# Last batch of a feature attention and gated MLP: sums of squares at fixed addresses, last output product in fp32 halves

## The chip, the cores and the metric

One core of one Trainium2 chip. The metric is the device time of one execution in microseconds. Five engines work beside each other, each through its own instructions in order: PE (TensorE, matrix products from SBUF into PSUM banks), PEld (its loads of the stationary operand), DVE (VectorE), ACT (ScalarE), POOL (GpSimd), and SP (SyncE), which issues the transfers.

## What is computed

For 4 batches of 1088 rows: an attention with products of features, 4 heads of 32 columns, and behind it a gated MLP. Cut to what matters:

```python
def phi(x):                                  # r = 8, so 64 features
    a = einsum('rd,bhsd->bhsr', S1, x)
    b = einsum('rd,bhsd->bhsr', S2, x)
    return einsum('bhsi,bhsj->bhsij', a, b).reshape(..., 64)
kv = einsum('bhsf,bhsd->bhfd', phi(k), v)
z = sum(phi(k), axis=2)
x = einsum('bhsf,bhfd->bhsd', phi(q), kv) / (einsum('bhsf,bhf->bhs', phi(q), z)[..., None] + 1e-6)

h = maximum(x @ w_in, 0)                     # 128 -> 1024
u, v = h[..., :512], h[..., 512:]
v_n = (v - mean(v)) / sqrt(var(v) + 1e-6)
v_s = einsum('ts,bsd->btd', w_spatial, v_n) + b_spatial[None, :, None]
out = (u * v_s) @ w_out                      # 512 -> 128
```

## The kernel before

**Precision.** Nearly every fp32 operand is split into a high part and a low rest, both of the type fp32r, and a product is three fp32r products, hi·hi, lo·hi and hi·lo (mm3, lines 441 to 444). The split of a tile is a cast on ACT (line 521) and a difference on DVE (line 452) or POOL (line 455). Weights arrive as 64-bit floating numbers and are brought to fp32 by from_f64 (from line 485), one step on ACT and six on a vector engine.

**Stages.** The kernel runs attention(b) (line 716), hidden_v (line 789: the half v, normed, as vh, vl and a rest v9) and main(b) (line 847) for the four batches, overlapping. main works on blocks (d, c): d is one of ND = 4 groups of 128 of the 512 columns, c one of three pieces of the 1088 rows, PIECES = 424, 332 and 332 columns wide, which stand in wTh and wTl at columns 0, 448 and 780. A block has its half u (bank pu, line 948), the product with w_spatial (nine steps of 128 rows, line 963 and those behind it, in a bank sp), the gate (a DVE product, line 1000, then the split into g, or xh and xl, or r) and out_mm (line 926), which adds the block's part of the output into a bank po of its piece. When the four d are summed, the bank is copied and stored. PSUM has three po banks, two sp, one pu and two sd.

**The last batch.** It runs in the order (0,0), (1,0), (2,0), quad 0, quad 2, (3,0). quad(d0) (line 1121) computes the 2 x 2 blocks of d0 and d0+1 and pieces 1 and 2 with seven products in place of eight, from sums of parts of w_spatial (w_sums, line 1033; its 16 parts are loaded again) and sums of parts of v (s_stores, s_sums, from line 1075, numbered 1 to 4). prod, line 1147, is the PE product with them, 12 instructions each, 14 of them: 168 instructions. plus (line 1155) and more add banks and kept sums on DVE.

**Order.** The code lists operations; Order.schedule (from line 190) sorts them on each engine from due times that run back from the end, taking away an entry of the table LEADS (line 66) for each operation. Tiles of a tag share a few buffers in a fixed turn (SB_BUFS), so an operation can wait until the tile that had its buffer is done with. HOMES (line 51) lists, in groups, the order in which the buffers lie in SBUF; two of its groups begin at an address of 0 and 64 modulo 256 bytes. In the products of prod, vh, vl, wih and wil stand at 64, and wTh, wTl, xh, xl, c and r at 0; kp, kt, v and pl stand where they come to lie.

**The end.** In before, the last block (3,0) ends with the gate (DVE, 424 columns), the cast to g (ACT), the difference (DVE), three fp32r products of 424 columns into po, a copy (ACT, line 937) and the store (SP, line 942).

Of the kernel before, what the change touches and what calls it, by code (L numbers as in the profile page):

```python
# [19 lines left out]
P = 128  # L20
# [3 lines left out]
ND = DH // P  # L24
# [27 lines left out]
    ("eps", "mask_sb", "sk", "bh", "bl", "sm", "st", "mv", "abT", "ka", "u", "vt", "kp", "kt", "v", "pl"),  # L52
    (0, "wTh", "wTl", "xh", "xl", "g", "c", "r", "b32"),
    (64, "vh", "vl", "v9", "wih", "wil", "woh", "wol", "kvh", "kvl"),
# [314 lines left out]
def tile_kernel(ctx: ExitStack, tc: tile.TileContext, kT, qT, vA, sks, idn, msk, wT, w_in, w_out, bsp, out):  # L369
# [35 lines left out]
    def reserve():  # L405

        at, base = 1024 + 4 * 32, None

        def up(n):
            return -(-n // 32) * 32  # L410

        for group in HOMES:
            if not isinstance(group[0], str):
                base = at if base is None else base
# [70 lines left out]
    def from_f64(x32, raw, n):  # L485
# [31 lines left out]
        step(c1, lambda v: v.tensor_tensor(out=x(), in0=x(), in1=ev(), op=ALU.add), [(x32, "e")], [(x32, "x")])  # L517
# [271 lines left out]
    def hidden_v(b, st, g):  # L789
# [46 lines left out]
        small(lambda: nm.ap, lambda: mv[:, :, 0], -sign, lambda: rs.ap, ALU.mult, ALU.mult, [mv, rs], [nm])  # L836
        for t in range(3):
            def dve(t=t):
                v.tensor_scalar(out=vt[:, t], in0=vt[:, t], scalar1=mv[:, t, 0:1], scalar2=rs[:, t:t + 1], op0=ALU.add if by_act else ALU.subtract, op1=ALU.mult)  # L839

            def act(t=t):
                nc.scalar.activation(vt[:, t], vt[:, t], AF.Identity, bias=nm[:, t:t + 1], scale=rs[:, t:t + 1])

            op("DVE", c_dve2(DH, True), dve, r=[mv, rs, nm], w=[(vt, t)], sh=True, alts=[("ACT", c_act(DH, ptr=True), act)], kind=f"norm{b}")


    def main(b, st):
        po, sums = [None] * 3, [0] * 3
        wide = b == B - 1
# [73 lines left out]
        def out_mm(d, c, hi, lo, parts):  # L923
            c0, cw = cols[c]
            if po[c] is None:
                po[c] = bank("po", f"po{b}{c}")
            o = po[c]
            sums[c] += 1
            first, end = sums[c] == 1, sums[c] == ND
            op("PE", c_mm(cw, 3), lambda: mm3(o[:, :cw], woh[:, d], wol[:, d], hi(), lo(), start=first, stop=end), r=[*parts, woh, wol], w=[o], due=due(c_mm(cw, 3)))  # L930
            if end:
                ob = tl("vt" if wide else "kp" if big(c) else "u", f"ob{b}{c}", [P, cw])
                late = due(0)

                def copy(eng, at, n, key):
                    if eng == "ACT":
                        op("ACT", c_act(n, True), lambda: nc.scalar.copy(out=ob[:, at:at + n], in_=o[:, at:at + n]), r=[o], w=[(ob, key)], due=late, lead=-8000)
                    else:
                        op("DVE", c_dve(n), lambda: nc.vector.tensor_copy(out=ob[:, at:at + n], in_=o[:, at:at + n]), r=[o], w=[(ob, key)], due=late, lead=-8000)

                def store(at, n, r):
                    op("SP", 470, lambda: nc.sync.dma_start(out=out[b, :, c0 + at:c0 + at + n], in_=ob[:, at:at + n]), r=r, kb=n // 2, due=late, lead=-12000)


                copy("DVE" if wide and c == 1 else "ACT", 0, cw, 0)
                store(0, cw, [ob])
# [51 lines left out]
        def gate(d, c, sp, u):  # L998
            cw = cols[c][1]
            op("DVE", c_dve(cw), lambda: nc.vector.tensor_tensor(out=u.ap, in0=sp[:, :cw], in1=u.ap, op=ALU.mult), r=[sp], w=[u], lead=LEAD[1])  # L1000
            if big(c):
                g = tl(("xh", "xl")[d % 2], f"g{b}{d}{c}", [P, 2, WIDE], F32R)
                parts = [(lambda: g[:, 0, :cw], (g, 0)), (lambda: g[:, 1, :cw], (g, 1))]
            else:
                tag = "r" if last(d, c) else "g"
                gh, gl = tl(tag, f"gh{b}{d}{c}", [P, cw], F32R), tl(tag, f"gl{b}{d}{c}", [P, cw], F32R)
                parts = [(lambda: gh.ap, gh), (lambda: gl.ap, gl)]
            (hi, wh), (lo, wl) = parts
            split(hi, lo, lambda: u.ap, cw, [u], [wh], [wl])
# [79 lines left out]
        def s_sums(d0, stores):  # L1089
# [7 lines left out]
            for m in range(2):  # L1097
# [3 lines left out]
                def own(t, at):  # L1101
                    return (lambda: t[:, at]), t
# [149 lines left out]
        for args in late:  # L1252
            out_mm(*args)
# [78 lines left out]
```

## Time and profile before

| what | us |
|---|---|
| three runs | 337.47, 330.95, 329.16; median 330.95 |
| the profiled execution | 329.36 |
| its span | 327.6 |
| PE busy in the span | 320.1 (98%) |
| DVE, ACT, POOL busy | 229.7, 166.7, 66.9 |
| granted clock of TensorE | 0.999 of full speed |

The times of the rows count from the span's start; 1.76 us of the execution lie outside the span. In a row, the number behind the start is the duration, and brackets give how long the engine had been idle before and what released it.

### The profile page before, as it was taken

The page shows a single profiled execution, that of the slowest core. Times are in us where ns is not written, and L with a number is a line of the kernel's source. Part 1 is how long each engine was busy: PE and PEld are TensorE (multiplying, and loading weights), DVE is VectorE, ACT ScalarE, POOL GpSimd, SP SyncE. Part 2 cuts the span into 40 slices and gives each one's busy share as a digit, 9 for nine tenths or more (in the row PEclk, how much of TensorE's full clock was granted, in tenths as well). Part 3 has the DMA queues.
Part 4 walks back from the last instruction along what each step waited for, and adds up shares of the span by engine and source line. Part 5 has one row for each costly group of instructions (what it writes and reads, how often), then busy time and mean ns, then how long its engine had stood idle before and what let it go on. Part 6 is the DMA issues. An engine that isn't in the chain of part 4 may idle for free.

```text
span 327.6 us, 6711 instructions
## 1 busy us (share of the span) xinstructions
PE 320.1 (98%) x2579; PEld 304.0 (93%) x2579; DVE 229.7 (70%) x503; ACT 166.7 (51%) x390; POOL 66.9 (20%) x83
## 2 busy tenths in 40 slices
PE   8999999999999999999999999999999999999995
PEld 7887988899999899999899999999999999999994
DVE  4899997444699973689976579899325777267281
ACT  2589656535674654576535476552424554153241
POOL 1000011685111025420102902156000013012000
PEclk9999999999999999999999999999999999999999
DMA  7932149764020274101044214000000231000001
GB/s 192 329 102 68 53 138 306 236 191 136 3 69 20 52 247 140 42 2 48 21 123 128 62 46 147 3 15 29 0 2 0 83 112 42 0 3 0 0 3 68
DMA packets 21260, 26.69 MB, mean 81 GB/s; under 512 B 2796, under 2 KB 20972, under 8 KB 21228
## 3 DMA queue, kind: packets, MB, share of 16 engines
q1 hardware_dynamic: 21228, 26.26, 26.1%
q8 instruction: 20, 0.33, 0.4%
q14 instruction: 12, 0.10, 0.1%
HBM read 23.18 MB, written 3.06 MB: 80 GB/s over the span
## 4 chain that ended last, share of the span: by engine, by line
PE 77%; DVE 9%; DMA 7%; ACT 3%; SPq 2%; issue 1%; DVEq 0%
PE sp L963 16%; PE sp L965 14%; PE sp L972 14%; PE sd L1147 4%; DMA v<-in_vA 3%; PE sp L1147 3%; DMA pl<-in_wT 3%; PE sd L442 3%; PE sd L444 3%; PE sd L443 3%; PE pu L442 2%; PE po L443 2%; PE pu L443 2%; PE pu L444 2%; PE sp L974 2%; PE po L442 2%
## 5 line engine op out<-in xcount | busy, mean ns | idle before, releaser
L963 PE MATMUL sp<-wTh,vh 128*128 128x332 f32 (+1 forms) x350 | 114.7, 328 | 0.0
L965 PE MATMUL sp<-wTh,vl 128*128 128x332 f32 (+1 forms) x304 | 99.0, 326 | 0.0
L972 PE MATMUL sp<-wTl,vh 128*128 128x332 f32 (+1 forms) x304 | 97.1, 326 | 0.0
L963 PEld LDWEIGHTS sp<-wTh,vh 128*128 128x128 f32 x350 | 65.8, 188 | 2.1 <-issue 1.0
L965 PEld LDWEIGHTS sp<-wTh,vl 128*128 128x128 f32 x304 | 57.2, 188 | 0.6
L972 PEld LDWEIGHTS sp<-wTl,vh 128*128 128x128 f32 x304 | 57.1, 188 | 0.1
L1000 DVE TENSOR_TENSOR u<-sp,u 128x332 f32<-128x332 f32 (+1 forms) x44 | 23.0, 522 | 23.6 <-PE sp L974 17.2
L521 ACT CAST g<-u 128x332 fp32r<-128x332 f32 (+1 forms) x42 | 20.5, 490 | 34.5 <-DVE u L1000 18.5
L452 DVE TENSOR_TENSOR g<-u,g 128x332 fp32r<-128x332 f32 (+1 forms) x42 | 24.2, 576 | 18.4 <-PE po L443 11.6
L777 DVE RECIPROCAL c<-c 128x384 f32<-128x384 f32 (+1 forms) x9 | 21.8, 2418 | 17.5 <-ACT c L775 17.5
L955 ACT ACTIVATE u<-pu 128x332 f32<-128x332 f32 (+1 forms) x44 | 20.6, 468 | 24.0 <-PE pu L444 19.4
L879 ACT CAST vh<-vt 128x384 fp32r<-128x384 f32 x36 | 17.6, 511 | 17.4 <-DVE vt L839 8.5
L803 DVE BATCH_NORM_STATS2 st<-vt 128x6 f32<-128x512 f32 x36 | 24.3, 686 | 1.9 <-ACT vt L801 1.4
L455 POOL TENSOR_TENSOR r<-pl,r 128x384 fp32r<-128x384 f32 (+1 forms) x18 | 17.6, 985 | 39.0 <-ACT r L521 30.1
L801 ACT ACTIVATE vt<-sd 128x512 f32<-128x512 f32 x36 | 21.3, 599 | 6.6 <-PE sd L444 5.8
L746 POOL TENSOR_TENSOR pl<-pl,pl 128x384 f32<-128x384 f32 (+1 forms) x18 | 17.6, 988 | 33.7 <-DMA pl<-qd 31.7
L881 DVE TENSOR_TENSOR vl<-vt,vh 128x384 fp32r<-128x384 f32 (+1 forms) x36 | 19.1, 540 | 7.5 <-ACT vh L879 7.4
L442 PE MATMUL pu<-xh,wih 128*128 128x332 f32 (+1 forms) x48 | 16.3, 339 | 0.7 <-ACT kp L955 0.6
L565 ACT CAST wTh<-pl 128x332 fp32r<-128x332 f32 (+1 forms) x27 | 13.0, 497 | 7.6 <-DMA pl<-in_wT 7.3
L839 DVE TENSOR_SCALAR vt<-vt,mv,sm 128x512 f32<-128x512 f32 x33 | 16.2, 540 | 0.0
L443 PE MATMUL pu<-xl,wih 128*128 128x332 f32 (+1 forms) x48 | 15.7, 328 | 0.0
L444 PE MATMUL pu<-xh,wil 128*128 128x332 f32 (+1 forms) x48 | 15.7, 328 | 0.0
(249 smaller groups left out, 633.6 us busy)
## 6 DMA issues: line engine op xcount, KB each, us to landing
pl<-in_wT SPq DMA_DIRECT2D x34, 166.0 KB
v<-in_vA SPq DMA_DIRECT2D x12, 198.0 KB
kt<-in_kT SPq DMA_DIRECT2D x12, 192.0 KB
pl<-qd SPq DMA_DIRECT2D x12, 192.0 KB
pl<-qd SPq DMA_DIRECT2D x24, 96.0 KB
pl<-in_wT SPq DMA_DIRECT2D x9, 212.0 KB
c<-in_qT SPq DMA_DIRECT2D x9, 192.0 KB
out<-u SPq DMA_DIRECT2D x6, 166.0 KB
```

Of the source, the lines that this page charges most:

```text
L442: nc.tensor.matmul(o, ah, bh, start=start, stop=False)
L443: nc.tensor.matmul(o, ah, bl, start=False, stop=False)
L444: nc.tensor.matmul(o, al, bh, start=False, stop=stop)
L452: return lambda: nc.vector.tensor_tensor(out=o(), in0=a(), in1=bb(), op=ALU.subtract)
L777: op("DVE", 135 + 6.3 * n, lambda x32=x32, n=n: nc.vector.reciprocal(out=x32[:, :n], in_=x32[:, :n]), w=[x32])
L801: op("ACT", c_act(512, True), lambda pv=pv, t=t: nc.scalar.activation(vt[:, t], pv.ap, AF.Relu), r=[pv], w=[(vt, t)])
L803: op("DVE", 690, lambda stats=stats, t=t: nc.vector.bn_stats(out=stats.ap, in_=vt[:, t]), r=[(vt, t)], w=[stats])
L963: nc.tensor.matmul(sp[:, :cw], vh[:, kt], wTh[:, kt, cs], start=(kt == begin), stop=False)
L965: nc.tensor.matmul(sp[:, :cw], vl[:, kt], wTh[:, kt, cs], start=False, stop=False)
L972: nc.tensor.matmul(sp[:, :cw], vh[:, kt], wTl[:, kt, cs], start=False, stop=False)
L1000: op("DVE", c_dve(cw), lambda: nc.vector.tensor_tensor(out=u.ap, in0=sp[:, :cw], in1=u.ap, op=ALU.mult), r=[sp], w=[u], lead=LEAD[1])
L1147: nc.tensor.matmul(x[:, :cw], p, q, start=i == 0 and n == 0, stop=end and i == 3 and n == 2)
```

## The change

**Addresses.** All sums of the quads are to lie at fixed places modulo 256 bytes. pl moves to the end of the group at 64. The tiles of the w_spatial sums move: t3l and two of t4h into thirds of xh and xl, the rest of t4h and t4l into kp, and t3h3 into a slot of v at a shifted column. The sums of v get three sets of four places: the second halves of wih and wil, vh and vl of d = 1, and two slots each of pl and v, used from a shifted column on. Since there are fewer places, sums 1, 2 and 4 of a quad are made first and sum 3 only behind product p5 (third).

**The last output product.** The bank po of piece 0 closes after three of four d, and ACT copies it into ob early. The last 128 rows of w_out are loaded once more and brought to whole fp32 (plain_wo). Behind the last block the gate is made in two halves of 212 columns, each is the moving operand of one fp32 product in a bank sd of its own, DVE adds the bank to ob, and each half is stored by itself (out_last).

**Order.** 412 entries of LEADS that belong to the last batch change: 300 have another value, 50 go, 62 are new.

```diff
-    ("eps", "mask_sb", "sk", "bh", "bl", "sm", "st", "mv", "abT", "ka", "u", "vt", "kp", "kt", "v", "pl"),
+    ("eps", "mask_sb", "sk", "bh", "bl", "sm", "st", "mv", "abT", "ka", "u", "vt", "kp", "kt", "v"),
-    (64, "vh", "vl", "v9", "wih", "wil", "woh", "wol", "kvh", "kvl"),
+    (64, "vh", "vl", "v9", "wih", "wil", "woh", "wol", "kvh", "kvl", "pl"),
...
-LEADS = {... 'po30:1': -16920, ... 'sp330:1': -119210, ...
+LEADS = {... 'po30:1': 42200, ... 'sp330:1': 32680, ... 'pl212:1': 120030, ... 'wo_x3:2': -50390, ...
+LAST = B - 1, ND - 1, 0
+TAIL = (0, 212), (212, 212)
...
-            first, end = sums[c] == 1, sums[c] == ND
+            first, end = sums[c] == 1, sums[c] == ND - (wide and c == 0)
...
+                if wide and c == 0:
+                    obs[c] = ob
+                    return
                 store(0, cw, [ob])
...
+        def out_last(ob, sp, u):
+            for at, n in TAIL:
+                op("DVE", c_dve(n), lambda at=at, n=n: nc.vector.tensor_tensor(out=u[:, at:at + n], in0=sp[:, at:at + n], in1=u[:, at:at + n], op=ALU.mult), r=[sp], w=[(u, at)], due=due(0))
+            for at, n in TAIL:
+                x = bank("sd", f"pl{at}")
+                op("PE", 14 + 4 * n / 2.4, f4=True, fn=lambda x=x, at=at, n=n: nc.tensor.matmul(x[:, :n], last_wo.ap, u[:, at:at + n], start=True, stop=True), r=[(u, at), last_wo], w=[x], due=due(3 * n / 2.4))
+                op("DVE", c_dve(n), lambda x=x, at=at, n=n: nc.vector.tensor_tensor(out=ob[:, at:at + n], in0=x[:, :n], in1=ob[:, at:at + n], op=ALU.add), r=[x], w=[(ob, at)], due=due(0), lead=-8000)
+                op("SP", 470, lambda at=at, n=n: nc.sync.dma_start(out=out[b, :, at:at + n], in_=ob[:, at:at + n]), r=[(ob, at)], kb=n // 2, due=due(0), lead=-12000)
...
+        def plain_wo():
+            raw, x, w = tl("pl", "wo_raw3", [P, 2 * DM]), tl("pl", "wo_x3", [P, 2 * DM]), tl("abT", "wo3", [P, DM])
+            load(raw, lambda: raw.ap.bitcast(U32), w_out[DFF // 2 - DM:, :].bitcast(U32), 131, after=AFTER_T)
+            from_f64(x, raw, DM, lambda: w.ap, w)
+            return w
...
-            t3h = [small("kt", f"t3h{i}") if i < 3 else small("v", "t3h3") for i in range(4)]
-            t3l = [small("v", f"t3l{i}") if i < 2 else third(i + 2) for i in range(4)]
-            t4h = [third(i if i < 3 else 3) for i in range(4)]
+            kps = [tl("kp", f"tkp{j}", [P, 2, 384], F32R) for j in range(3)]
+            t3h = [small("kt", f"t3h{i}") if i < 3 else shifted("t3h3") for i in range(4)]
+            t3l = [third(i) for i in range(4)]
+            t4h = [third(4 + i) if i < 2 else part(i - 2) for i in range(4)]
+            t4l = [part(2 + i) for i in range(4)]
...
-            kps = [tl("kp", f"skp{j}", [P, 3, 2, P], F32R) for j in range(3)]
+            for j in range(4):
+                t = tl("pl" if j < 2 else "v", f"ss{j}", [P, 384 if j < 2 else 396], F32R)
+                def place(t=t):
+                    at = (-1696 * t.slot if t.tag == "pl" else 64 - 1584 * t.slot) % 256 // 4
+                    return t[:, at:at + 256].rearrange("p (t m) -> p t m", m=P)
...
+            for m in range(2):
+                sums(m, ("1", "2", "4"))
+            def third():
+                for m in range(2):
+                    sums(m, ("3",))
+            return ss, third
...
             e5 = keep("e5", alone("p5", sum_a("1"), sum_b(1)))
+            third()
```

Where the instructions move, in three places. In the rows a number behind a name is the buffer; lines of the changed kernel are two to six higher for the same code, and 15 and more from w_sums on.

ACT in the main part of batch 0. wTh<-pl are casts of w_spatial as it is loaded, g, xh and xl are the high halves of gates. Before:

```order
L565 CAST wTh<-pl_101 128x332
L565 CAST wTh<-pl_102 128x332
L565 CAST wTh<-pl_104 128x332
L565 CAST wTh<-pl_103 128x332
L521 CAST g_111<-u_87 128x332
L565 CAST wTh<-pl_100 128x332
L521 CAST xh_108<-kp_95 128x424
L565 CAST wTh<-pl_99 128x332
L521 CAST xl_110<-kp_94 128x424
```

The same place of ACT after the change:

```order
L567 CAST wTh<-pl_129 128x332
L567 CAST wTh<-pl_133 128x332
L961 ACTIVATE u_87<-pu_204 128x332
L567 CAST wTh<-pl_135 128x332
L523 CAST g_105<-u_87 128x332
L567 CAST wTh<-pl_130 128x332
L523 CAST xh_102<-kp_95 128x424
L567 CAST wTh<-pl_132 128x332
L523 CAST xl_104<-kp_94 128x424
L567 CAST wTh<-pl_131 128x332
```

Of the 18 casts of w_spatial of these two pieces, 15, 16 and 17 stood ahead of g, xh and xl; now 14, 15 and 16 do.

DVE at the first quad. pl_102<-pl_102,pl_103 are sums of w_spatial parts, vl and vh rests of the normed v, g the rest of a gate, u_88<-sp the next gate. Before:

```order
L1025 TENSOR_TENSOR pl_104<-pl_102,pl_104 128x332
L881 TENSOR_TENSOR vl<-vt_91,vh 128x256
L1025 TENSOR_TENSOR pl_102<-pl_102,pl_103 128x332
L888 TENSOR_TENSOR vh<-vt_91,vh 64x128
L452 TENSOR_TENSOR g_111<-u_87,g_112 128x332
L1000 TENSOR_TENSOR u_88<-sp_367,u_88 128x332
```

The same place of DVE after the change, where lines 509 to 519 are the steps that make fp32 of w_out's last rows:

```order
L509 TENSOR_SCALAR pl_135<-pl_135 128x128
L1040 TENSOR_TENSOR pl_131<-pl_131,pl_133 128x332
L511 TENSOR_SCALAR pl_135<-pl_135 128x128
L1040 TENSOR_TENSOR xl_103<-pl_130,v 128x332
L1040 TENSOR_TENSOR kp_2920<-pl_131,kp_2914 128x332
L512 SCALAR_TENSOR_TENSOR pl_135<-pl_132,pl_135 128x128
L884 TENSOR_TENSOR vl<-vt_92,vh 128x384
L517 TENSOR_SCALAR pl_135<-pl_135 128x128
L454 TENSOR_TENSOR g_105<-u_87,g_106 128x332
L518 SCALAR_TENSOR_TENSOR pl_135<-pl_132,pl_135 128x128
L1006 TENSOR_TENSOR u_88<-sp_368,u_88 128x332
L519 TENSOR_TENSOR abT_83<-pl_135 128x128
```

Four of the six steps on w_out now stand ahead of the rest of the gate, and five ahead of the next gate.

PE at the end of the kernel. po, sp and sd are PSUM banks, r and g the halves of gates. Before:

```order
L442 MATMUL po_313<-r_120,woh 128x332
L443 MATMUL po_313<-r_121,woh 128x332
L444 MATMUL po_313<-r_120,wol 128x332
L442 MATMUL po_324<-g_113,woh 128x424
L443 MATMUL po_324<-g_111,woh 128x424
L444 MATMUL po_324<-g_113,wol 128x424
```

The last five products of PE after the change:

```order
L444 MATMUL po_314<-r_114,woh 128x332
L445 MATMUL po_314<-r_115,woh 128x332
L446 MATMUL po_314<-r_114,wol 128x332
L1025 MATMUL sd_145<-u_89,abT_83 128x212
L1025 MATMUL sd_175<-u_89,abT_83 128x212
```

Two fp32 products, which read the gate u itself, stand in the place of three fp32r products that read its halves.

## Rows read from the trace of the kernel before

**Rows 1.** The page: busy time of the engines and the chain that ended last.

```profile
PE 320.1 (98%) x2579; PEld 304.0 (93%) x2579; DVE 229.7 (70%) x503; ACT 166.7 (51%) x390; POOL 66.9 (20%) x83
...
PE 77%; DVE 9%; DMA 7%; ACT 3%; SPq 2%; issue 1%; DVEq 0%
```

**Rows 2.** Windows: us, PE, PEld, DVE, ACT, POOL busy (x instructions), PEclk, DMA share, GB/s.

```profile
265.00:325.00 60.00, 58.64 (x356) 57.12 (x354) 34.23 (x73) 22.51 (x53) 6.89 (x11) 1.00 0.05 19
325.30:326.20 0.90, 0.00 (x0) 0.00 (x0) 0.00 (x0) 0.00 (x0) 0.00 (x0) 1.00 0.64 241
326.20:327.60 1.40, 0.00 (x0) 0.00 (x0) 0.00 (x0) 0.00 (x0) 0.00 (x0) 0.86 0.00 0
```

**Rows 3.** Timeline of the end: start, us, engine, line, output and inputs.

```profile
321.52 0.60 DVE L1000 TENSOR_TENSOR u<-sp,u 128x424 f32<-128x424 f32 x1 [2.37 <-PE sp L974]
...
322.15 0.55 ACT L521 CAST g<-u 128x424 fp32r<-128x424 f32 x1 [3.58 <-DVE u L1000]
...
322.51 0.31 PE L444 MATMUL po<-r,wol 128*128 128x332 f32 x1
...
322.74 0.60 DVE L452 TENSOR_TENSOR g<-u,g 128x424 fp32r<-128x424 f32 x1 [0.20 <-ACT g L521]
...
323.39 0.46 PE L443 MATMUL po<-g,woh 128*128 128x424 f32 x1 [0.17 <-DVE g L452]
...
323.68 0.35 PE L444 MATMUL po<-g,wol 128*128 128x424 f32 x1
324.07 0.51 ACT L937 COPY vt<-po 128x424 f32<-128x424 f32 x1 [0.78 <-PE po L444]
```

**Rows 4.** Timeline of ACT, then of PE's weight loads, in batch 0.

```profile
58.23 0.47 ACT L565 CAST wTh<-pl 128x332 fp32r<-128x332 f32 x1 [2.79 <-DMA pl<-in_wT]
...
62.04 0.47 ACT L521 CAST g<-u 128x332 fp32r<-128x332 f32 x1
...
63.10 0.19 PEld L443 LDWEIGHTS po<-g,woh 128*128 128x128 f32 x1 [0.35 <-DVE g L452]
...
64.51 0.19 PEld L443 LDWEIGHTS po<-xh,woh 128*128 128x128 f32 x1 [0.51 <-DVE xh L452]
...
65.72 0.19 PEld L443 LDWEIGHTS po<-xl,woh 128*128 128x128 f32 x1 [0.72 <-DVE xl L452]
```

**Rows 5.** Timeline of DVE and PE at the first quad.

```profile
268.51 1.10 DVE L452 TENSOR_TENSOR g<-u,g 128x332 fp32r<-128x332 f32 x1
...
269.14 0.31 PE L442 MATMUL po<-g,woh 128*128 128x332 f32 x1
...
269.54 0.49 DVE L1000 TENSOR_TENSOR u<-sp,u 128x332 f32<-128x332 f32 x1
...
269.67 0.42 PE L443 MATMUL po<-g,woh 128*128 128x332 f32 x1 [0.22 <-DVE g L452]
...
269.92 0.32 PE L444 MATMUL po<-g,wol 128*128 128x332 f32 x1
```

**Rows 6.** Timeline of PE around fp32 products of batch 1's attention.

```profile
107.56 0.39 PE L443 MATMUL sd<-wil,xh 128*128 128x512 f32 x1
107.79 0.40 PE L444 MATMUL sd<-wih,xl 128*128 128x512 f32 x1
108.12 0.55 PE L731 MATMUL sd<-c,sk 128*64 128x192 f32 x4
108.59 0.42 PE L963 MATMUL sp<-wTh,vh 128*128 128x332 f32 x1
```

**Rows 7.** Timeline of PE at two places of the quads.

```profile
279.74 0.31 PE L1147 MATMUL sd<-r,wih 128*128 128x332 f32 x1
...
280.62 0.35 PE L442 MATMUL po<-g,woh 128*128 128x424 f32 x1
...
291.00 0.47 PE L1147 MATMUL sd<-wTh,kp 128*128 128x332 f32 x2
...
291.92 0.32 PE L442 MATMUL pu<-xh,wih 128*128 128x332 f32 x1
```

More of the change, by code (lines that the diff above doesn't have):

```diff
@@ L413, in reserve @@
             if not isinstance(group[0], str):
-                base = at if base is None else base
+                base = -(-at // 256) * 256 if base is None else base
                 pad = (base + group[0] - at) % 256
@@ L483, in tile_kernel, with from_f64 @@
     NSK = 2 * H * R
-    def from_f64(x32, raw, n):
+    def from_f64(x32, raw, n, out=None, w_out=None):
         def w(i):
@@ L516, in from_f64 @@
         step(c1, lambda v: v.scalar_tensor_tensor(out=ev(), in0=w(0), scalar=2.0 ** -52, in1=ev(), op0=ALU.mult, op1=ALU.mult), [raw], [(x32, "e")])
-        step(c1, lambda v: v.tensor_tensor(out=x(), in0=x(), in1=ev(), op=ALU.add), [(x32, "e")], [(x32, "x")])
+        step(c1, lambda v: v.tensor_tensor(out=out() if out else x(), in0=x(), in1=ev(), op=ALU.add), [(x32, "e"), (x32, "x")], [w_out or (x32, "x")])
     def split(hi, lo, x, n, r, wh, wl, pool=False, due=None, alt=False):
@@ L848, in main @@
         po, sums = [None] * 3, [0] * 3
+        last_wo, obs = None, {}
         wide = b == B - 1
@@ L1041, in small, with shifted, hi @@
                 return lambda: t.ap, (t, None)
+            def shifted(name):
+                t = tl("v", name, [P, 396], F32R)
+                def hi():
+                    t.ap
+                    at = -1584 * t.slot % 256 // 4
+                    return t[:, at:at + cw]
+                return hi, (t, None)
             wide_x = [tl(tag, f"t{tag}", [P, 3, 384], F32R) for tag in ("xh", "xl")]
@@ L1075, in s_stores @@
         def s_stores():
-            kps = [tl("kp", f"skp{j}", [P, 3, 2, P], F32R) for j in range(3)]
-            places = [(lambda t=t, m=m: t[:, m], [(t, m)]) for t in kps for m in range(3)]
+            places = []
             for w in (wih, wil):
@@ L1081, in s_stores @@
                     places.append((lambda w=w, m=m: w[:, DH + 256 * m:DH + 256 * m + 256].rearrange("p (t m) -> p t m", m=P), [(w, (1, 0)), (w, ("s", m))]))
-            vh, vl = hl[1][:2]
-            places.append((lambda: vh[:, 0:2], [(vh, 0)]))
-            places.append((lambda: vl[:, 0:2], [(vl, 0)]))
-            places.append((lambda: vh[:, 2:4], [(vh, 0), (vh, 1)]))
-            names = [f"{n}{p}{m}" for n in "1423" for p in "hl" for m in range(2)]
-            return dict(zip(names, places))
+            for v, _ in ((hl[1][0], 0), (hl[1][1], 0)):
+                places.append((lambda v=v: v[:, 0:2], [(v, 0)]))
+                places.append((lambda v=v: v[:, 2:4], [(v, 0), (v, 1)]))
+            for j in range(4):
+                t = tl("pl" if j < 2 else "v", f"ss{j}", [P, 384 if j < 2 else 396], F32R)
+                def place(t=t):
+                    t.ap
+                    at = (-1696 * t.slot if t.tag == "pl" else 64 - 1584 * t.slot) % 256 // 4
+                    return t[:, at:at + 256].rearrange("p (t m) -> p t m", m=P)
+                places.append((place, [(t, None)]))
+            return [dict(zip([f"{p}{m}" for p in "hl" for m in range(2)], x)) for x in (places[:4], places[8:], places[4:8])]
         def s_sums(d0, stores):
+            which = dict(zip("1342", (0, 0, 1, 2) if d0 == 0 else (1, 1, 2, 0)))
             def v(d, kt, n=1):
@@ L1096, in s_sums, with sums, own @@
             ss = {}
-            for m in range(2):
+            def sums(m, ns):
                 parts = [(0, 2)] if m == 0 else [(2, 1), (3, 1)]
-                x, y = (tl(tag, f"{tag}s{d0}{m}", [P, 2, P]) for tag in ("kvh", "kvl"))
-                def own(t, at):
-                    return (lambda: t[:, at]), t
-                def step(n, t, get, add=False):
+                x = tl("kvh" if len(ns) > 1 else "kvl", f"s{ns[0]}{d0}{m}", [P, 2, P])
+                def own(at):
+                    return (lambda: x[:, at]), x
+                for n in ns:
@@ L1105, in step @@
                     for i, w in parts:
                         at = slice(i - 2 * m, i - 2 * m + w)
-                        (a, ra), (bb, rb) = get(i, w, at)
-                        sub_any(own(t, at)[0], a, bb, w * P, [ra, rb], [(t, (i, w))], add)
-                    (hi, wh), (lo, wl) = stores[f"{n}h{m}"], stores[f"{n}l{m}"]
-                    full = own(t, slice(0, 2))[0]
-                    op("ACT", c_act(256), lambda: nc.scalar.copy(out=hi(), in_=full()), r=[t], w=wh)
-                    sub_any(lo, full, lambda: hi().bitcast(F32), 256, [t, *wh], wl)
@@ L1113, in step @@
-                    ss[n, m] = hi, wh, lo, wl
-                step("1", x, lambda i, w, at: (v(d1, i, w), v(d1, i + 4, w)), True)
-                step("3", y, lambda i, w, at: (v(d0, i, w), v(d1, i, w)))
-                step("2", x, lambda i, w, at: (own(x, at), v(d0, i, w)))
-                step("4", x, lambda i, w, at: (v(d0, i + 4, w), own(x, at)))
-            return ss
+                        (p, rp), (q, rq) = {
+                            "1": lambda: (v(d1, i, w), v(d1, i + 4, w)),
+                            "2": lambda: (own(at), v(d0, i, w)),
+                            "4": lambda: (v(d0, i + 4, w), own(at)),
+                            "3": lambda: (v(d0, i, w), v(d1, i, w)),
+                        }[n]()
@@ new lines, in sums @@
+                        sub_any(lambda at=at: x[:, at], p, q, w * P, [rp, rq], [(x, (i, w))], n == "1")
+                    (hi, wh), (lo, wl) = (stores[which[n]][f"{p}{m}"] for p in "hl")
+                    op("ACT", c_act(256), lambda hi=hi: nc.scalar.copy(out=hi(), in_=x.ap), r=[x], w=wh)
+                    sub_any(lo, lambda: x.ap, lambda hi=hi: hi().bitcast(F32), 256, [x, *wh], wl)
+                    ss[n, m] = hi, wh, lo, wl
+            for m in range(2):
+                sums(m, ("1", "2", "4"))
@@ L1121, in quad @@
+            def third():
+                for m in range(2):
+                    k.part = ("S", f"S{d0}")
+                    sums(m, ("3",))
+            return ss, third
         def quad(d0, ts, stores):
             k.part = ("S", f"S{d0}")
-            ss = s_sums(d0, stores)
+            ss, third = s_sums(d0, stores)
             k.part = ("m",)
@@ L1227, in main @@
             ts = w_sums()
+            last_wo = plain_wo()
             stores = s_stores()
@@ L1239, in main @@
                     spatial(d, c, sp, kt)
+                if x == plan[-1]:
+                    end = sp, u
+                    continue
                 gated(d, c, sp, u)
@@ L1253, in main @@
             out_mm(*args)
+        if wide:
+            out_last(obs[0], *end)
     sts = [{} for _ in range(B)]
```

8 lines of the change are left out of this document (6 added, 2 removed).

## The prediction

> **What bounds the kernel now.** I read the page first, then the lists of what PE waited for, then the timeline at each of those places. The page gives PE 320.1 of 327.6 us and puts 77% of the last-ending chain on PE [rows 1]; no other engine is above 70%. In the stretch in which the last batch runs, 265 to 325 us, PE is busy for 58.64 of 60.00 us while VectorE has 34.23 us of work [rows 2]. So a microsecond is gained in three ways only: fewer or shorter PE instructions, a PE stall that goes, or a shorter end behind the last product. The profiled execution took 329.36 us: the span of 327.6 plus 1.76 outside it. The sum below stands on that execution; the median of the three runs, 330.95, lies 1.6 above it.
>
> **1. The end of the kernel.** In the trace of before, PE issues its last free product at 322.51, and from there a chain runs alone: gate 321.52 (0.60), ACT's cast 322.15 (0.55), VectorE's difference 322.74 (0.60), then the two products that wait for it at 323.39 and 323.68, then ACT's copy 324.07 to 324.58 [rows 3]. The store's packets move from about 325.3 to 326.2, and nothing is transferred in the last 1.4 us [rows 2].
> After the change the cast and the difference are gone. The halves of the gate cost about 0.37 us each: a product of 424 columns takes 0.60 (321.52 [rows 3]) and one of 332 columns 0.49 (269.54 [rows 5]), which is 1.2 ns a column and 0.09 at the start, so 0.35 for 212. Both are done about 322.25, before PE is free at 322.51 + 0.15 = 322.66. So nothing waits for them, unless they are late by over 0.4.
> The fp32 product has no row of its own shape. The nearest is the group at line 731: the PE product ahead of it starts at 107.79 and needs 0.23 (the pitch of its kind, 107.56 to 107.79), so PE is free at 108.02; the group starts at 108.12, 0.10 later, and the next fp32r product at 108.59 [rows 6]. So the switch costs 0.10 and the 192 columns 0.47, of which 0.10 is the switch back: 0.37, and 0.37 x 212/192 = 0.41. The group holds two products of 64 output rows each. If they took turns, one costs half, 0.20; if they ran side by side, one costs all of it. I take 0.41; the row's own busy time of 0.55 is the upper bound.
> PE then issues until 322.66 + 0.10 + 2 x 0.41 = 323.58. Behind a last product its reader starts 0.39 after the start (323.68 to 324.07 [rows 3]), 0.19 of it the issue of 424 columns (332 take 0.88/6 = 0.147 [rows 7], times 424/332), so 0.20 after the issue ends: 323.78. The addition of 212 columns costs 0.35 again: 324.13, against 324.58. That is 0.45. The first half's store is issued 0.41 ahead of it, and the second moves 109 KB where the whole moved 217 (241 GB/s for 0.90 us [rows 2]): 0.45 less if size were all, of which I count 0.25. **Term 1: -0.7.** Ends: with 0.20 a product and all of the transfer, -1.3; with 0.55 a product and a store that gains nothing, -0.2; a second store whose completion adds as much as the halving gives, +0.2.
>
> **2. Casts of batch 0.** The PE weight loads for the output product at 63.10, 64.51 and 65.72 sat idle 0.35, 0.51 and 0.72 us, each released by VectorE's difference of a gate [rows 4]. VectorE had waited for ACT's casts, and ACT takes its queue in order: the cast of g stands at 62.04, behind casts of w_spatial, the first of which waited 2.79 us for a load at 58.23 [rows 4]. By the order g, xh and xl stand behind one w_spatial cast fewer than before. One cast is 0.47 us (58.23 [rows 4]). If all three gates come 0.47 earlier, the three waits fall by 0.35, 0.47 and 0.47 if each were alone; they follow one another, and a PE that is let go sooner comes sooner to the next wait, so the gain is that of the last place, at most about one cast: **term 2: -0.4.** Ends: 0, where the load is what ends the wait in any order; -1.2, where two of the waits go.
>
> **3. The first quad.** At 269.14 PE issues the first of the three products with g and the second only at 269.67, where 0.15 would do: 0.38 lost, and 0.10 more to the one behind it. It waited for VectorE's difference at 268.51, which took 1.10 us and to which VectorE came late, from other work: its row names no idle time before it [rows 5]. In the changed order this difference has one vl operation and short steps ahead of it, and three wide `pu` products (424 columns, 0.19 each) more on PE's side. **Term 3: -0.5**, the whole stall. Ends: 0 if the difference still takes 1.10 and comes last, -0.6 with the gaps around it.
>
> **4. The addresses.** Six products with both operands at fixed places modulo 256 go from 279.74 to 280.62, 0.88 us; six with kp as the stationary operand, whose place is not fixed, from 291.00 to 291.92, 0.92 [rows 7]. That is 0.04/6, about 7 ns each. The 14 quad products are 168 instructions; 56 of them, by the order, hold kp in the kernel before. 56 x 6 ns: **term 4: -0.3.** Ends: 0, and 168 x 6 ns = -1.0 if each of them were slowed now.
> The Trainium skill says otherwise, in "SBUF — State Buffer", section "SBUF: two separate sides": among the engines only the port pair that VectorE and GpSimd share makes anyone wait, and PE never waits. By that, addresses are worth nothing and the sum is 328.1; the 0.04 us in the rows speak mildly against it, at the resolution of 0.01.
>
> **5. New tight places.** The sums "3" move behind p5 and the PE order is another. Bank sp of the first piece is written again ten PE products (about 1.5 us) after its last use; in between stand an addition and a gate on VectorE, 0.49 each (269.54 [rows 5]), and twice the handover of 0.20 from term 1, 1.4 us. The turn of an sd bank in the same quad has about 1.0. Each holds with no more than 0.1 to spare, or fails by a few tenths: **term 5: +0.3.** Ends 0 and +1.0.
>
> **Counted at nothing:** the six steps that turn the last 128 rows of w_out into fp32 (128 columns each, under half of the 0.49 for 332 [rows 5], so under 1.5 us together), since VectorE is idle for 25 of 60 us there [rows 2], and the load of 131 KB. Without that cover they are the rival A. The longer waits for v and pl places, shared now with the sums, are counted with term 5.
>
> Sum: 329.36 - 0.7 - 0.4 - 0.5 - 0.3 + 0.3 = **327.8 us**.
>
> **Rivals.**
> A, slower: the w_out load is the last of the 17 reloads and its tile is one that the w_spatial sums must free first; VectorE, in order, then stands at its first step with the gate's difference and the gate of the next bank behind it, as the order shows. PE needs both. The price is a load come late, as at 58.23, 2.79 us [rows 4]; it decides if the load lands after about 267. Terms 1, 2, 4 and 5 stay, term 3 goes: 329.36 - 0.7 - 0.4 - 0.3 + 0.3 + 2.8 = 331.1. For it: a real queue in order with no other way round. Against: DMA is busy for 5% in that stretch [rows 2].
> B, no net change: the stalls only move. PE waits for the same loads of batch 0 at other instructions (term 2 nothing), the g difference stays long (term 3 nothing), and term 5 costs 0.5; with term 1 at -0.5 and term 4 at -0.2 that is 329.2. For it: PE is busy at 98% [rows 1], so what is saved in one stage can wait in the next.
> C, the addresses do nothing, whether because PE is never held up or because the change doesn't do what it says: the third piece's moving columns begin at column 780, 3120 bytes, which is 48 modulo 256, so the weights are not all at one distance from their partner. All else as forecast: 328.1.
>
> **How the numbers follow.** The forecast has 0.45; A 0.15; B 0.2; C 0.2. The likeliest gives 327.8. All good ends together are 329.36 - 1.3 - 1.2 - 0.6 - 1.0 + 0 = 325.3, which needs five lucky ends at once; the range goes down to 325.6. Upward it takes in A's 331.1 and a little for a median that lies over the profiled execution, as before's does by 1.6: 331.4. A measurement of this kernel can tell about 2% from no change, 6.6 us. No case above reaches -6.6, and A would need its wait more than twice: faster 0.03, within 0.94, slower 0.03.
>
> **What would show it.** Term 1: two fp32 products about 0.4 apart directly behind the last fp32r product, no cast or difference behind the gate, and about 2.8 us from the end of the last addition to the end of the span, where ACT's last copy has 3.0 now (324.58 to 327.6). Term 2: idle before the three weight loads near 63 to 66 us down by 0.4 in sum or more. Term 3: no wait for the g difference at the first `po` product of the first quad. Term 4: 0.88 for six quad products everywhere. Term 5: PE waiting for VectorE at the restart of an sp or sd bank. A: VectorE idle at the first w_out step with a DMA named. The prediction is wrong if PE's idle time in the last 65 us grows, or if the fp32 products take 0.6 us or more each.

## The result, and the profile after

The changed kernel takes 326.86 us (median; 326.04 the shortest), where the runs of before on the same chip have 330.5. The ratio is 0.9908, with a 95% interval of 0.9883 to 0.9933: 3.0 us faster. The forecast was 327.8 with a range of 325.6 to 331.4, within 2%. The profiled execution took 326.74, its span 325.0, which is 2.6 us under the span of before; the stages below divide these 2.6 us. Ratios leave out executions with a lower granted clock (about 0.97), and the profiles of experiments 1, 6 and 10 fell in such, so of these three only the times are used.

The page of the changed kernel, in the lines that answer to [rows 1]:

```profile
PE 318.4 (98%) x2580; PEld 303.7 (93%) x2580; DVE 228.6 (70%) x513; ACT 166.1 (51%) x390; POOL 64.6 (20%) x81
...
PE 81%; DVE 8%; DMA 5%; ACT 3%; SPq 2%; issue 1%; ACTq 0%
```

PE is busy for 98% as before, and in less time; its share of the chain rose from 77% to 81%, since waits went. To see where, I take four PE products with the same work before them in both orders, and read the time between. Timeline of PE, kernel before:

```profile
45.25 0.35 PE L963 MATMUL sp<-wTh,vh 128*128 128x424 f32 x1
...
78.56 0.31 PE L963 MATMUL sp<-wTh,vh 128*128 128x332 f32 x1
...
266.58 0.31 PE L974 MATMUL sp<-wTl,v 66*128 66x332 f32 x1
...
321.13 0.35 PE L974 MATMUL sp<-wTl,v 66*128 66x424 f32 x1
```

The same four products in the changed kernel:

```profile
45.12 0.35 PE L969 MATMUL sp<-wTh,vh 128*128 128x424 f32 x1
...
76.68 0.31 PE L969 MATMUL sp<-wTh,vh 128*128 128x332 f32 x1
...
265.20 0.31 PE L980 MATMUL sp<-wTl,v 66*128 66x332 f32 x1
...
319.15 0.35 PE L980 MATMUL sp<-wTl,v 66*128 66x424 f32 x1
```

The starts of these rows and the ends of the spans (to two decimals 327.58, 324.96, 326.31, 326.75 and 326.52) give the stages. The last three columns are kernels of the experiments (2, 12 and 11), read at the same four products.

| stage | before | changed | before with the new early order | changed with the old early order | changed with the old end |
|---|---|---|---|---|---|
| start to first row | 45.25 | 45.12 | 45.91 | 45.32 | 46.30 |
| to the second: main part of batch 0 | 33.31 | 31.56 | 31.59 | 33.59 | 31.73 |
| to the third: batches 1 and 2 | 188.02 | 188.52 | 187.78 | 188.10 | 188.30 |
| to the fourth: last batch | 54.55 | 53.95 | 54.56 | 53.93 | 53.71 |
| to the end of the span | 6.45 | 5.81 | 6.47 | 5.81 | 6.48 |

Changed against before: -0.13, -1.75, +0.50, -0.60, -0.64, together -2.62. Two thirds came in batch 0, where none of the change's three parts lies. The third row of the table differs by 0.4 us between kernels that all have the changed kernel's order there (188.52 here, 188.54 in experiment 4, 188.12 in experiment 8), so its +0.50 is not read as a cost of the change.

**Batch 0.** What PE's weight loads waited for between 45 and 67 us (sum, times, longest), kernel before:

```profile
PEld po L443 <- DVE xl L452: 0.7, 1, 0.7
PEld pu L442 <- ACT kp L955: 0.7, 1, 0.7
PEld po L443 <- DVE xh L452: 0.5, 1, 0.5
PEld po L972 <- DVE wTl L568: 0.4, 1, 0.4
PEld po L443 <- DVE g L452: 0.4, 1, 0.4
PEld sd L591 <- issue: 0.3, 1, 0.3
```

and the changed kernel:

```profile
PEld po L445 <- DVE xh L454: 0.8, 1, 0.8
PEld sd L593 <- DMA pl<-in_wT: 0.2, 1, 0.2
```

The waits for g and xl of [rows 4] are gone; that for xh is longer (0.8 for 0.5). Gone too are two that the prediction did not name: 0.7 for ACT's kp (a hidden product that stood too early in PE's order) and 0.4 for a rest of w_spatial (wTl).

**Last batch.** Window of the changed kernel, columns as in [rows 2]:

```profile
265.00:320.50 55.50, 55.50 (x343) 55.14 (x342) 33.59 (x81) 21.61 (x53) 6.60 (x12) 1.00 0.03 11
```

PE is busy for all of 55.50 us. In before the stage from 266.57 to 321.12 has 54.33 of 54.55. The lists name no wait of PE in this stretch that took the place of the one in [rows 5]; idle times too short for the lists come with experiments 3 and 11.

At the first quad, timeline of DVE and PE, against [rows 5]:

```profile
267.52 0.49 DVE L454 TENSOR_TENSOR g<-u,g 128x332 fp32r<-128x332 f32 x1
...
268.26 0.31 PE L444 MATMUL po<-g,woh 128*128 128x332 f32 x1
268.40 0.31 PE L445 MATMUL po<-g,woh 128*128 128x332 f32 x1
268.55 0.31 PE L446 MATMUL po<-g,wol 128*128 128x332 f32 x1
```

The difference takes 0.49 us, not 1.10, and is done at 268.01; PE comes to the product at 268.26 and goes on 0.14 later, with no bracket on the row. In before, POOL worked on a sum of w_spatial beside the difference, from 268.24 to 269.24:

```profile
268.24 1.00 POOL L1025 TENSOR_TENSOR pl<-pl,pl 128x332 f32<-128x332 f32 x1 [39.44 <-DVE pl L1025]
```

In the changed kernel POOL has no instruction from 266.01 to 270. A DVE sum of 332 columns that does stand beside one of POOL there (265.16, POOL's from 265.12 to 266.01) takes 1.22 us, where others of its kind take 0.49.

**The end.** Timeline of the changed kernel, against [rows 3]:

```profile
319.54 0.66 DVE L1022 TENSOR_TENSOR u<-sp,u 128x212 f32<-128x212 f32 x2 [2.37 <-PE sp L980]
...
320.53 0.32 PE L446 MATMUL po<-r,wol 128*128 128x332 f32 x1
320.68 0.88 PE L1025 MATMUL sd<-u,abT 128*128 128x212 f32 x4
...
321.24 0.74 DVE L1026 TENSOR_TENSOR vt<-sd,vt 128x212 f32<-128x212 f32 x2 [0.62 <-PE sd L1025]
...
321.77 0.38 SPq L1027 DMA_DIRECT2D out<-vt  x1
322.24 0.40 SPq L1027 DMA_DIRECT2D out<-vt  x1
```

From the last free product (320.53 here, 322.51 in [rows 3]) to the end of the span it is 4.43 us, before 5.07. (The expectations below have 4.47 and 5.1, from spans to one decimal.) The first fp32 product starts 0.15 behind the last fp32r one, the usual pitch. The addition waits for the first product until 321.24, then both additions run to 321.98. The second store is issued only at 322.24, 0.26 behind its addition.

### The profile page after: what moved, and what is told of

The parts are those of the page before. It is cut to its first block, busy times and chain, and to the rows that moved or that the text cites. A ratio compares the mean times of both kernels' runs of the same rounds, so it can differ in the third digit from the quotient of the medians.

```text
span 325.0 us, 6726 instructions
## 1 busy us (share of the span) xinstructions
PE 318.4 (98%) x2580; PEld 303.7 (93%) x2580; DVE 228.6 (70%) x513; ACT 166.1 (51%) x390; POOL 64.6 (20%) x81
## 3 DMA queue, kind: packets, MB, share of 16 engines
HBM read 23.31 MB, written 3.06 MB: 81 GB/s over the span
## 4 chain that ended last, share of the span: by engine, by line
PE 81%; DVE 8%; DMA 5%; ACT 3%; SPq 2%; issue 1%; ACTq 0%
PE sp L969 16%; PE sp L971 14%; PE sp L978 14%; PE sd L1203 4%; PE sp L1203 3%; PE sd L444 3%; PE sd L445 3%; PE sd L446 3%; PE pu L444 2%; PE po L445 2%; PE po L444 2%; DMA pl<-in_wT 2%; PE po L446 2%; PE sp L980 2%; PE pu L445 2%; PE pu L446 2%
## 5 line engine op out<-in xcount | busy, mean ns | idle before, releaser
L523 ACT CAST g<-u 128x332 fp32r<-128x332 f32 (+1 forms) x41 | 19.8, 490 | 31.9 <-DVE u L1006 21.6
L1006 DVE TENSOR_TENSOR u<-sp,u 128x332 f32<-128x332 f32 (+1 forms) x43 | 22.3, 520 | 19.1 <-PE sp L980 12.6
L884 DVE TENSOR_TENSOR vl<-vt,vh 128x384 fp32r<-128x384 f32 (+1 forms) x36 | 17.8, 505 | 5.3 <-ACT vh L882 5.2
L570 POOL TENSOR_TENSOR wTl<-pl,wTh 128x332 fp32r<-128x332 f32 (+1 forms) x9 | 8.2, 935 | 55.5 <-ACT wTh L567 52.6
```

## The experiments

Some kernels put instructions in a given order. For that the planner takes a list of operations first, in the place of its own choice:

```diff
+            if prefix:
+                o, fe = prefix.pop()
+                s = max(free[fe], self.ready_at(o, fe))
...
+                best, forced = (s, fe, o), True
-            for e, os in avail.items():
+            for e, os in ({} if best else avail).items():
```

The old-end, one-piece, late-hidden and two-queue kernels use the same list, holding the changed kernel's own order, so that nothing moves but what the diff says.

**1 and 12. The changed kernel with the old order of the first 100 us.** The list is the first 663 operations of before's order, then the rest of the changed kernel's.

> The changed kernel, with the operations of the first 100 us (by the planner's clock) put in the order of the kernel before; everything later in the order of the change. Theory (order): between 45 and 67 us the changed kernel gained 1.5 us on PE only because instructions of batch 0 stand in another order, so with the old order PE reaches the same product near 66.7 us instead of 64.9 and the span is about 325.0 + 1.6 = 326.6; the waits at about 46.7, 51.0 and 62 to 66 us are back. Rival (loads): these waits differ from one execution to the next with the arrival of loads; then the span stays at 325.0 and the waits fall at other places.

> The changed kernel with the old order of the first 100 us once more (the edit is that of the first run), for a trace at the full clock. Theory (order): 1.6 us above the changed kernel, and the waits of the kernel before near 46.7, 51.0 and 62 to 66 us are back in the trace. Rival (loads): neither.

The first gave a ratio to before of 0.9972 (0.9954 to 0.9990), median 329.51. The second gave 0.9966 (0.9949 to 0.9982), with the stages of the table: 33.59 us in batch 0, before's 33.31, and the changed kernel's 53.93 and 5.81 in the last two. Its waits between 45 and 67 us:

```profile
PEld po L460 <- DVE xl L469: 0.7, 1, 0.7
PEld pu L459 <- ACT kp L976: 0.7, 1, 0.7
PEld po L460 <- DVE xh L469: 0.6, 1, 0.6
PEld po L993 <- DVE wTl L585: 0.4, 1, 0.4
PEld po L460 <- DVE g L469: 0.4, 1, 0.4
PEld sd L608 <- issue: 0.3, 1, 0.3
PEld po L459 <- ACT g L538: 0.2, 1, 0.2
```

These are the six of before, and one more. The order of batch 0 is worth 2.0 us of this kernel's 33.59, and by the ratios 0.9966 to 0.9908 some 1.9.

**2. Before with the new order of the first 100 us.**

> The kernel before, with the operations of the first 100 us (by the planner's clock) put in the order of the changed kernel, nothing else of the change. Theory (order): PE reaches the product that stood at 66.7 us at about 65.0; span about 327.6 - 1.6 = 326.0, more than half of the whole gain without any of the change's three parts. Rival (loads): no difference, 327.6.

Ratio 0.9926 (0.9900 to 0.9952): 2.4 us faster than before with none of the three parts. Its waits are the changed kernel's two:

```profile
PEld po L458 <- DVE xh L467: 0.8, 1, 0.8
PEld sd L606 <- DMA pl<-in_wT: 0.2, 1, 0.2
```

Batch 0 takes 31.59 us, and the last batch and the end stay as in before, 54.56 and 6.47. So the order theory holds in both directions. All traces bear it out: the nine in the new order have 31.0 to 32.0 us in batch 0, the two in the old 33.3 and 33.6, and the load theory falls. Which of the moved instructions of batch 0 matter was not taken apart further. What does differ from one execution to the next is the first stage: 45.1 to 46.5 us in the nine traces of the new order, 45.3 in both of the old; whether the order has a part in that, these traces can't tell.

**3 and 11. The old end.** The diff of the end is undone, the order of the rest kept:

```diff
-            last_wo = plain_wo()
...
-                if x == plan[-1]:
-                    end = sp, u
-                    continue
                 gated(d, c, sp, u)
```

> The changed kernel without the fp32 end: the last block's gate is split by a cast and a difference, three fp32r products of 424 columns go into the po bank with the other three d, one copy and one store; the load and the six steps on w_out go. Theory (the end is worth what its rows say, 0.6 us): span 325.0 + 0.6 = 325.6, and the distance from the start of the last free fp32r product to the end of the span goes from 4.47 to about 5.1 us. Rival (the early load and the steps on w_out cost as much as the end gains): 325.0 or less, with PE earlier at the last free product.

> The changed kernel without the fp32 end once more (the edit is that of the run with the old end), timed beside the changed kernel. Theory (the end is worth its 0.6 us also in the time): 0.6 us above the changed kernel. Rival (the load of w_out and its six steps take it back elsewhere): the same time within 0.3 us, and PE then reaches the last free product 0.5 us earlier than in the changed kernel, counted from the same product at 77 us.

From the last free product to the end: 319.86 to 324.95 and 321.42 to 326.52, 5.09 and 5.10 us, so the new end is worth 0.66 by itself. But the stage ahead of it is shorter without the load and the six steps: 53.71 in the second and 318.48 - 264.71 = 53.77 in the first, against 53.95 in the changed kernel, 53.93 in that with the old early order and 319.33 - 265.43 = 53.90 in that of experiment 9. About 0.2 us goes back there. Half of it has a place in the changed kernel's rows:

```profile
267.94 0.28 DVE L518 SCALAR_TENSOR_TENSOR pl<-pl,pl 128x128 f32<-128x128 uint32 x1
268.14 0.49 DVE L1006 TENSOR_TENSOR u<-sp,u 128x332 f32<-128x332 f32 x1
...
268.70 0.45 PE L969 MATMUL sp<-wTh,vh 128*128 128x424 f32 x1
268.98 0.36 PE L971 MATMUL sp<-wTh,vl 128*128 128x424 f32 x1
```

The product at 268.70 is the first into a bank sp that DVE's gate has to read out first. A step on w_out (267.94) stands ahead of that gate, the gate ends at 268.63, and the next product of PE comes 0.28 behind the first, where 0.19 is the pitch. In both kernels with the old end these two products are 0.19 apart. The other 0.1 is spread over all products, and is of the size by which executions of one order differ in this stage.

The second expectation's rival has PE at the last free product 0.5 earlier, counted from the product at 77 us. It is 0.46 in the second kernel and 0.32 in the first, of which 0.22 and 0.14 lie in batches 1 and 2, so the rival's way of counting overstates what goes back. The times can't settle the rest, some 0.4 us: ratios 0.9903 (0.9883 to 0.9923) and 0.9917 (0.9888 to 0.9947), beside the changed kernel's 0.9908 and, again in experiment 10, 0.9895 (0.9863 to 0.9928).

> The changed kernel itself once more, beside the others on the same chip. Its ratio to before is 0.991 as measured; the waits of PE from 36 us on stand where they stood (0.77 us between 36 and 60 us, 0.24 behind 264.5), whereas those before 36 us, which hang on the first loads, may differ by some 0.5 us.

Of this expectation only the ratio was seen, and it holds.

**4. One product, one addition, one store.**

```diff
-TAIL = (0, 212), (212, 212)
+TAIL = ((0, 424),)
```

> The changed kernel with the last product as one fp32 product of 424 columns, one addition and one store, in place of two halves. Theory (the halves matter by the addition and the bytes): the addition of 424 columns ends 0.25 later and the store moves all bytes behind it, 0.25 more: the last free product to the end is 4.47 + 0.5 = 5.0 us. Rival (the fp32 product is the whole gain): 4.5 to 4.6 us, since two halves cost a second issue and a second addition.

```profile
321.20 0.32 PE L461 MATMUL po<-r,wol 128*128 128x332 f32 x1
321.36 0.87 PE L1040 MATMUL sd<-u,abT 128*128 128x424 f32 x2
...
322.27 0.60 DVE L1041 TENSOR_TENSOR vt<-sd,vt 128x424 f32<-128x424 f32 x1 [1.04 <-PE sd L1040]
...
322.90 0.33 SPq L1042 DMA_DIRECT2D out<-vt  x1
```

The addition ends at 322.87, 1.67 us behind the last free product (1.45 with halves), and the store leaves at once, at 322.90. To the end of the span (325.81) it is 4.61 us against 4.43. So the halves are worth 0.18 and not 0.5: the rival. Ratio 0.9925 (0.9907 to 0.9942), no distance from the changed kernel's that the intervals can hold.

**9. The first half's store from ACT.**

```diff
-                op("SP", 470, lambda at=at, n=n: nc.sync.dma_start(out=out[b, :, at:at + n], in_=ob[:, at:at + n]), r=[(ob, at)], kb=n // 2, due=due(0), lead=-12000)
+                q, eng = (nc.scalar, "ACT") if at == 0 else (nc.sync, "SP")
+                op(eng, 470, lambda at=at, n=n, q=q: q.dma_start(out=out[b, :, at:at + n], in_=ob[:, at:at + n]), r=[(ob, at)], kb=n // 2, due=due(0), lead=-12000)
```

> The changed kernel with the first half's store issued by ACT, in place of SP; the second half's stays on SP. Theory (SP's queue paces the end): in the changed kernel the second addition ended at 321.98 and its store was issued only at 322.24, since SP issues one store after the other, 0.42 to 0.47 us apart; with ACT's queue for the first half it is issued at once, and the last free product to the end of the span takes 4.47 - 0.25 = 4.2 us. Rival (the transfers themselves pace the end): 4.4 to 4.5 us.

```profile
320.71 0.32 PE L461 MATMUL po<-r,wol 128*128 128x332 f32 x1
...
321.78 0.38 DVE L1041 TENSOR_TENSOR vt<-sd,vt 128x212 f32<-128x212 f32 x1
321.83 0.37 ACTq L1043 DMA_DIRECT2D out<-vt  x1
322.19 0.33 SPq L1043 DMA_DIRECT2D out<-vt  x1
```

Now the second store follows its addition (321.78 + 0.38) by 0.03 us, where it followed by 0.26. It leaves 1.48 us behind the last free product, where it was 1.71. But from 320.71 to the end (325.04) it is 4.33 us, only 0.10 less than in the changed kernel: neither the 4.2 of the theory nor the 4.4 of the rival. From the second store's issue to the end it is now 2.85 us, where it was 2.72. The two transfers run closer together: the busy share of the DMA engines is 1.03 from 322.6 to 323.4, where the changed kernel has 0.97, 0.91 and 0.63 in the 1.2 us from 322.2. So the queue of SP held the second store back by 0.23, and by this one trace 0.13 of it is lost again behind the issue. Ratio 0.9902 (0.9878 to 0.9926): by its trace the shortest end of all, by its times not to be told from the changed kernel.

**5 and 6. The group of buffers at other addresses.**

```diff
-    (64, "vh", "vl", "v9", "wih", "wil", "woh", "wol", "kvh", "kvl", "pl"),
+    (128, "vh", "vl", "v9", "wih", "wil", "woh", "wol", "kvh", "kvl", "pl"),
```

> The changed kernel with the group of buffers that begins at 64 modulo 256 bytes (vh, vl, wih, wil, woh, pl and others) moved to 128; the order of all instructions is the same. Theory (addresses): the products whose two operands stand 64 apart now stand 128 apart; in the kernel before, products 112 or 160 apart took 4.5 to 5 ns more each than those 64 apart, so some 1,650 such products cost 7 us more: span 332. Rival (PE never waits for a place in SBUF): 325.0.

> The same with the group at 96. Theory (addresses): a cost between that of 64 and that of 112 apart, 2 to 4 ns more a product, 3 to 7 us: 328 to 332. Rival: 325.0.

With 128 the ratio is 1.0037 (1.0017 to 1.0056), 4.3 us above the changed kernel; with 96 it is 1.0014 (0.9997 to 1.0031), 3.5 us above. The instructions and their order are the same. The span with 128 is 330.04, which is 5.1 more, but 1.4 of that lie ahead of the first row of the table (46.51 for 45.12), where executions differ anyhow; the stages behind that row are 0.3, 2.6 and 0.8 longer and the end is the same, 3.7 together. The ten products of the changed kernel ahead of the row of 265.20 above begin at

```profile
263.73 0.31 PE L969 MATMUL sp<-wTh,vh 128*128 128x332 f32 x1
```

which is 1.47 us; the same ten with the group at 128 are

```profile
267.95 0.31 PE L969 MATMUL sp<-wTh,vh 128*128 128x332 f32 x1
...
269.46 0.32 PE L980 MATMUL sp<-wTl,v 66*128 66x332 f32 x1
```

1.51 us. From the starts of all products that follow each other without a wait, and the addresses of their two operands, the time of one above 146.5 ns (332 columns) or 187 ns (424 columns) is:

```
kernel        distance modulo 256   products   mean ns above
changed        64                   1057       2.1
changed        16                    355       3.7
changed       112                     41       6.8
changed       160                     43       7.3
group at 128  128                   1136       6.0
group at 128   80                    346       5.4
```

1,100 products at 3.9 ns more and 350 at 1.7 give 4.9 us for the whole kernel, where the times show 4.3. The 7 us expected were too many, since all 1,650 were counted at the higher price. So a place in SBUF does cost PE time on this chip. The distance alone does not set the price: the products 112 apart in the table, which have xh and xl moving and wih and wil stationary, cost 6.8 ns, while 24 others at the same distance in experiment 7 cost 4.7; what else of the two addresses counts was not tried.

The page "SBUF — State Buffer" of the Trainium skill says, in "SBUF: two separate sides", that PE never waits on anyone. It speaks there of ports that engines share; taken as the prediction took it, that places are worth nothing to PE, these runs do not agree, and they decide.

**7. Places of the quads' sums, 96 bytes on.**

```diff
-                    at = (-1696 * t.slot if t.tag == "pl" else 64 - 1584 * t.slot) % 256 // 4
+                    at = (-1696 * t.slot if t.tag == "pl" else 64 - 1584 * t.slot) % 256 // 4 + 24
```

> The changed kernel with the third set of places for the sums of v (pl and v) used 96 bytes further on; only these 36 quad products change their distance, from 64 to 160. Theory (addresses): these products take about 5 ns more each than the rest, 0.2 us in all. Rival: the same mean as before the shift, within 1 ns.

The 168 quad products together are 0.84 us above their shortest time, in the changed kernel 0.69 and in six others with its places 0.55 to 0.63. The sum rose by about the 0.2 us expected, but not in the products expected. Of the 36, only 12 went from 64 to 160 apart, and their mean rose from 3.3 to 6.7 ns. The other 24 are of the third piece; they went from 16 to 112 apart, and theirs fell from 5.8 to 4.7. All 36 together went from 5.0 to 5.4, which is the rival's "within 1 ns". The rest of the sum comes from the 132 products that kept their distance (3.9 to 4.9 ns), and why is open. So this run, a single one, shows the price in 12 products and not as a rule.

**8. The hidden products behind the output product.** In the list, pu300 goes behind po21.

> The changed kernel with the three hidden products of 424 columns at the first quad put behind the output product that waited in the kernel before (269.14 there), in place of ahead of it. Theory (cover): these 0.56 us of PE work are what hides the gate's difference; PE comes to the output product 0.56 earlier and waits 0.2 to 0.3 us for it. Rival (shorter queue on VectorE alone): the difference is ready anyway, and PE does not wait.

```profile
267.56 0.49 DVE L469 TENSOR_TENSOR g<-u,g 128x332 fp32r<-128x332 f32 x1
...
267.62 0.31 PE L459 MATMUL po<-g,woh 128*128 128x332 f32 x1
268.11 0.42 PE L460 MATMUL po<-g,woh 128*128 128x332 f32 x1 [0.17 <-DVE g L469]
268.36 0.31 PE L461 MATMUL po<-g,wol 128*128 128x332 f32 x1
```

PE reaches the output product at 267.62, which is 2.50 us behind the third of the four products (265.12 here), where it was 3.06: 0.56 earlier. It goes on only at 268.11: 0.34 lost above the pitch of 0.15, and 0.10 behind it. The difference again takes 0.49 and is done at 268.05. So the three hidden products are the cover, and without them most of the wait is back.

## Why the prediction held, and where it was off

- **Term 1, the end, -0.7: -0.64, and about 0.2 goes back.** Sizes in it were off in both directions and cancel; that the sum is so near is in part luck. The switch to fp32 costs nothing (0.15 from 320.53 to 320.68, counted 0.25), and a product takes 0.36, not 0.41: the first addition starts at 321.24, 0.56 behind the product's start, of which 0.20 is the handover. So the second addition ends 1.45 behind the last free product, where the text had 1.62. Against that, the second store was to follow its addition; SP issued its last three stores 0.42 and 0.47 us apart, and this one came 0.26 late (experiment 9). The six steps were counted at nothing; the old end shows 0.2 in the stage ahead, 0.10 of it at a bank that waits for DVE behind one of these steps.
- **Term 2, casts of batch 0, -0.4: mis-sized, since it took in one place of two.** From 58.79 to 66.66 before and 57.69 to 64.92 after, 7.87 and 7.23, the waits that the term spoke of gave 0.64. From the first row to there, 13.54 and 12.57, another 0.97 came from waits for kp and wTl. The step that failed is the reading of batch 0: I compared ACT's casts at the three gates and did not compare PE's order between 45 and 59 us, where the planner moved hidden products and attention work too.
- **Term 3, the first quad, -0.5: right in size, by two causes of which it named one.** With it the last batch lost 0.60 us. The cover that the term named is shown by experiment 8. But the cover alone would not have done: had the difference taken 1.10 us again from 267.52, it would have ended at 268.62, behind the 268.40 at which PE wants it. The term has that case as its end of 0. That the difference came down to 0.49, with POOL no longer at work beside it, was not foreseen.
- **Term 4, addresses, -0.3: -0.1 to -0.2.** The quad products are 0.87 and 0.86 us above their shortest time in the two kernels with the old places (before and experiment 2), 0.55 to 0.69 in seven with the new. Of the 0.87, 0.11 is no price of a place: at 287.27 in before a weight load stood idle for 0.10, and the next product came 0.25 behind instead of 0.15. The price of 6 to 7 ns for a product with kp was right (6.3 ns over 47 products, against 3.5 for those 64 apart); what was wrong is that the products 64 apart are not free.
- **Term 5, tight places, +0.3: next to nothing.** No wait of PE is listed from 265 to 320.5. The one place of the term's kind is the bank sp at 268.70, 0.10 late, and before had lost 0.11 at the same product (270.08).
- **Rivals.** A fell, though its wait is there: ACT, which makes the first step on w_out, stood idle 1.44 us for the load until 263.24. That is 4.3 us ahead of the gate's difference, DVE did not wait for the load, and the price of a late gate was not paid. B fell at the first quad and the end. C fell with experiments 5 and 6, as a rule; of the change's own quads, the third piece's 48 products, 16 apart, do stay at 4.9 ns, as C said.

The sum came to -1.6 and the span to -2.6. Batch 0 alone gave 1.35 more than its term; batches 1 and 2, for which nothing was counted, stand against it with their 0.50, and the other stages are within 0.15 of what was counted for them. So the range held, being 5.8 us wide, while most of the largest gain stood in no term.

## What to carry to other kernels

Where a planner sets the order from due times that run back from the end, an edit of the last stage can reorder the first one too, as here, where no entry of LEADS outside the last batch changed: compare the order of every stage, and time the order alone before a gain is put down to the edit. Here some 2 us of 3.0 are had by before's own instructions in another order. And where several stores end a kernel, the queue that issues them is a part of the end: the second half of a store waited 0.23 us for the one ahead. A second queue gave back 0.10 of that in one trace, too little for the times to show.

## What was not expected

Products whose operands stand 64 bytes apart modulo 256 are the fastest of all distances that occur here, 2.1 ns above the shortest time against 6.0 at 128 apart: about 4 us of 327 hang on where a group of buffers begins. And PE took up an fp32 product behind an fp32r one with no loss at the end (0.15 us from start to start), while [rows 6] show 0.10 us ahead of the fp32 group of the attention; which of the two is the rule was not tried.
